# Row, key and r transposes moved from TensorE to the DMA in an RWKV-5 + MLP kernel, with a new order

## Chip, cores and metric

One core of one Trainium2 chip. The metric is the device time of one launch in microseconds. Every instruction's place in its engine's queue is written out by hand in the program, so a time is the result of five queues that run side by side.

## What is computed

Two steps. The first is a linear recurrence (RWKV-5) over 768 positions for 4 batches and 8 heads of 48 channels; the second is a normalisation and a two-layer MLP on the resulting rows of 384 channels.

```python
batch, n_heads, seq, head_dim = (4, 8, 768, 48)
for t in range(S):
    kt, vt, rt = (k[:, :, t].copy(), v[:, :, t].copy(), r[:, :, t].copy())
    cur = np.einsum('bhd,bhe->bhde', u[None] * kt, vt)
    y[:, :, t] = np.einsum('bhd,bhde->bhe', rt, state + cur)
    state = w[None, :, :, None] * state + np.einsum('bhd,bhe->bhde', kt, vt)
...
x = np.ascontiguousarray(attn_out.transpose(0, 2, 1, 3)).reshape(B, S, H * D)
...
xn = (x - mu) / np.sqrt(var + 1e-06) * g_ln
ch = np.maximum(xn @ w_ch1, 0.0) @ w_ch2
return (x + ch).astype(np.float32)
```

Inputs and output are float32; the matrix products run in bf16.

## The kernel before

**Chunks.** The 768 positions of a batch are cut into 6 chunks of 128, so there are 24 chunks (numbered 0 to 23) and as many tiles of 128 rows for the MLP. Within a batch a chunk needs the state `Z` of the chunk before it.

**One chunk, first step.** `LK`, `LR`, `LV` load k, r and v (196.6 KB each, rows of 192 bytes) through SP's DMA queue into rings of ten buffers. `SK` and `SR` (on VectorE or GpSimd) multiply k and r by powers of w and give the bf16 tiles `sck` and `scr`; `CV` gives v in bf16. TensorE needs k and r with channels on the partitions: `TR` turns them, four 128x128 blocks each, into the PSUM tile `tr` (there is one of it, shared with `LT` below), and `TC`, `TCr` or `TCk` copy them to the tile `trs` (a ring of three). `AT` forms the score products, `AM` masks them, `Q` multiplies the turned r and k, `S` forms the state's increment, `ZU`/`ZD` update the state, `Y` forms the output of the chunk and `X` adds the diagonal part `VB`.

**One chunk, second step.** `ST` and `AG` give mean and variance, `XN` the centred row tile `xn` in bf16. `LT` turns it with three 128x128 transposes on TensorE and `XT` copies it to `xT`. Tiles go through the MLP in groups of one or two (`GROUPS`). `UP` is the first layer: for a group of one, 3 PSUM tiles of 12 products each with 128 columns; for a group of two, 6 PSUM tiles of 6 products each with 256 columns. `RL` takes the ReLU. `DN` is the second layer, 3 steps of 4 products with 384 columns for a tile (`DN,4i+d` is tile i, third d). `OT` scales and adds the residual, `STO` stores 196.6 KB through SP's queue.

**Weights.** `LW1,n` loads the third n of the first layer's weights (SP's queue); `SW` scales its three parts; `IW2,n` loads third n of the second layer's weights and converts it, issued from GpSimd's queue. `DN,d` for tile 0 is the first user of third d, so `DN,2` waits for `IW2,2`.

**Transposes by DMA.** For the chunks in `K_BY_DMA` (18 to 23) the k half of `TR` is left out and `TKD` turns `sck` (128x512) with one DMA transpose on SP's queue. `LTD` does the same for `xn` (128x384) but is not in the order before.

**Order.** `PLAN` is the whole schedule: each entry is a step, its index and its engine (v VectorE, s ScalarE, g GpSimd, - fixed). Each engine, and SP's DMA queue, takes its own entries strictly in this order, and a step waits for the data and the free buffers it needs. A DMA on SP's queue that waits keeps all later ones behind it waiting. `DU` and `WU` are products without use, 105 in all, that keep TensorE busy in the first 23 us.

The order before begins like this (up to `DN,2`):

```
MW,0,v WF,0,- TL,0,s MI,0,g MP,0,v WU,13,- MM,0,g LN,0,s LK,0,- ROWSI,0,s WBM,0,- LV,1,-
LR,0,- FK,0,s CV,1,v FR,0,s SK,0,v LK,1,- SR,0,g LR,1,- SK,1,v DU,18,- TR,0,- UW,0,g
WL,0,s LK,2,- SR,1,g TCk,0,s LR,2,- TCr,0,s SK,2,g Q,0,v DU,22,- TR,1,- LV,0,- AT,0,-
TCk,1,s SR,2,v LG,0,- LW1,2,- TCr,1,s AMa,0,v CV,0,g UGC,0,s AMb,0,v DU,13,- TR,2,- S,0,-
Q,1,v TC,2,s Y,0,- AT,1,- CC,0,v ZU,0,v LV,2,- AMa,1,v VB,0,g DU,3,- S,1,- SW,7,s
AMb,1,v LW1,1,- SW,8,s IW2,0,g X,0,v SW,6,s DU,13,- AT,2,- Q,2,v Y,1,- CV,2,g ST,0,v
AG,0,v LW1,0,- CC,1,s XN,0,s RS,0,g ZU,1,v SW,5,s SW,3,v DU,16,- LT,0,- VB,1,g XT,0,v
SW,4,s DU,6,- UP,2,- X,1,v S,2,- RL,2,s SW,2,g ST,1,v UP,1,- SW,0,s SW,1,v IW2,2,g
AG,1,v AM,2,v UP,0,- XN,1,s IW2,1,g LK,3,- LT,1,- RL,1,s CC,2,v XT,1,v LR,3,- DU,1,-
Y,2,- RL,0,s VB,2,g ZU,2,v UP,18,- SK,3,v LV,3,- DN,0,- SR,3,v RL,18,s UP,17,- X,2,v
TR,3,- CV,3,g ST,2,v RL,17,s UP,16,- RS,1,g TC,3,v AG,2,v RL,16,s Q,3,v AT,3,- XN,2,v
RS,2,g AM,3,v S,3,- LT,2,- DN,1,- XT,2,s CC,3,s UP,33,- ZU,3,v LK,4,- DN,2,- LV,6,-
```

Of the kernel before, what the change touches and what calls it, by code (L numbers as in the profile page):

```python
# [13 lines left out]
GROUPS = [1, 1, 1, 1, 1, 1, 1, 1, 2, 2, 2, 2, 2, 2, 1, 1, 1, 1]  # L14
ZPE = [1, 2, 3]
K_BY_DMA = [18, 19, 20, 21, 22, 23]
SLOTS = {'kf': 10, 'rf': 10, 'vf': 10, 'sck': 3, 'scr': 3, 'vv': 4, 'trs': 3, 'q': 2, 'A': 2, 'cc': 4, 'Z': 3, 'ZS': 2, 'Vb': 3, 'x': 13, 'xn': 3, 'xT': 4, 'hT': 4, 'ot': 3}
PLAN = """
MW,0,v WF,0,- TL,0,s MI,0,g MP,0,v WU,13,- MM,0,g LN,0,s LK,0,- ROWSI,0,s WBM,0,- LV,1,-
LR,0,- FK,0,s CV,1,v FR,0,s SK,0,v LK,1,- SR,0,g LR,1,- SK,1,v DU,18,- TR,0,- UW,0,g  # L20
WL,0,s LK,2,- SR,1,g TCk,0,s LR,2,- TCr,0,s SK,2,g Q,0,v DU,22,- TR,1,- LV,0,- AT,0,-
TCk,1,s SR,2,v LG,0,- LW1,2,- TCr,1,s AMa,0,v CV,0,g UGC,0,s AMb,0,v DU,13,- TR,2,- S,0,-
Q,1,v TC,2,s Y,0,- AT,1,- CC,0,v ZU,0,v LV,2,- AMa,1,v VB,0,g DU,3,- S,1,- SW,7,s
AMb,1,v LW1,1,- SW,8,s IW2,0,g X,0,v SW,6,s DU,13,- AT,2,- Q,2,v Y,1,- CV,2,g ST,0,v
AG,0,v LW1,0,- CC,1,s XN,0,s RS,0,g ZU,1,v SW,5,s SW,3,v DU,16,- LT,0,- VB,1,g XT,0,v
SW,4,s DU,6,- UP,2,- X,1,v S,2,- RL,2,s SW,2,g ST,1,v UP,1,- SW,0,s SW,1,v IW2,2,g
AG,1,v AM,2,v UP,0,- XN,1,s IW2,1,g LK,3,- LT,1,- RL,1,s CC,2,v XT,1,v LR,3,- DU,1,-
Y,2,- RL,0,s VB,2,g ZU,2,v UP,18,- SK,3,v LV,3,- DN,0,- SR,3,v RL,18,s UP,17,- X,2,v
TR,3,- CV,3,g ST,2,v RL,17,s UP,16,- RS,1,g TC,3,v AG,2,v RL,16,s Q,3,v AT,3,- XN,2,v
RS,2,g AM,3,v S,3,- LT,2,- DN,1,- XT,2,s CC,3,s UP,33,- ZU,3,v LK,4,- DN,2,- LV,6,-  # L30
VB,3,g UP,32,- OT,0,v Y,3,- SK,4,v LR,4,- DN,4,- RL,32,v RL,33,s DN,5,- CV,6,s LR,5,-
X,3,v SR,4,v DN,6,- LV,4,- ST,3,v TR,4,- SR,5,g UP,34,- OT,1,v LV,5,- TC,4,s AG,3,v
DN,8,- CV,4,v XN,3,g LK,5,- Q,4,v AT,4,- RL,34,s DN,9,- RS,3,g AM,4,v LK,7,- LT,3,-
S,4,- XT,3,s DN,10,- LK,6,- SK,5,v CC,4,s VB,4,g UP,48,- OT,2,v LR,10,- TR,5,- SK,7,v
UP,49,- SK,6,g ZU,4,v RL,48,s LR,6,- TC,5,v Y,4,- CV,5,s DN,12,- RL,49,v LR,12,- ZD,4,g
AT,5,- X,4,v DN,13,- AM,5,v LR,7,- SR,6,g UP,50,- LV,7,- ST,4,v TR,6,- RL,50,s Q,5,v
SR,7,g Y,5,- AG,4,v STO,1,- TC,6,v S,5,- XN,4,s DN,14,- STO,0,- CC,5,v CV,7,s Q,6,v
VB,5,g LT,4,- LV,11,- AT,6,- XT,4,v S,6,- OT,3,v UP,64,- LV,9,- X,5,v CC,6,s UP,66,-
RS,4,g ST,5,v RL,64,s LR,8,- TR,7,- AM,6,v RL,66,s UP,65,- SR,10,g CV,9,s LK,11,- DN,16,-
AG,5,v RL,65,s TC,7,v RS,5,g Y,6,- LR,9,- XN,5,s DN,17,- ZU,6,v VB,6,g Q,7,v LT,5,-  # L40
LK,8,- DN,18,- XT,5,s AT,7,- X,6,v LK,10,- UP,80,- ST,6,v S,7,- SR,8,v RL,80,s LR,14,-
UP,82,- SK,8,g AM,7,v UP,81,- RL,82,s LK,9,- TR,8,- CC,7,s AG,6,v OT,4,v RL,81,s RS,6,g
Y,7,- LK,14,- TC,8,v XN,6,s DN,20,- VB,7,g CV,11,s ZU,7,v LV,8,- LT,6,- DN,21,- Q,8,v
SR,9,g X,7,v XT,6,s AT,8,- LK,15,- SK,9,v DN,22,- CV,8,s UP,96,- ZD,7,g LV,13,- ST,7,v
AM,8,v TR,9,- RL,96,s SK,10,g STO,2,- S,8,- UP,97,- LR,11,- CC,8,s TC,9,v SR,12,g Y,8,-
OT,5,v RL,97,s TR,10,- STO,4,- Q,9,v AT,9,- VB,8,g LK,12,- TC,10,s AG,7,v UP,98,- ZU,8,v
AM,9,v ZD,8,g S,9,- LV,12,- XN,7,s DN,24,- CC,9,s LT,7,- Q,10,v SK,11,g LR,16,- DN,25,-
ZU,9,v RL,98,s X,8,v AT,10,- XT,7,s LV,15,- DN,26,- ZD,9,g ST,8,v UP,114,- AM,10,v LV,10,-
VB,9,g Y,9,- RL,114,s UP,113,- STO,3,- SR,11,g AG,8,v X,9,v XN,8,s LK,13,- UP,112,- CV,10,s
ST,9,v RS,7,g TR,11,- OT,6,v RL,112,s LR,17,- S,10,- AG,9,v TC,11,v RL,113,s SR,14,g Y,10,-  # L50
DN,28,- CC,10,s LR,15,- SK,13,v CV,12,s XN,9,s VB,10,g LT,8,- AT,11,- ZU,10,v LK,17,- DN,29,-
XT,8,s Q,11,v SK,12,g LT,9,- X,10,v DN,30,- LV,16,- XT,9,s AM,11,v S,11,- UP,130,- RS,8,g
LR,13,- UP,129,- CC,11,v OT,7,v RL,130,s ZD,10,g LK,21,- TR,12,- ST,10,v RL,129,s UP,132,- CV,13,v
VB,11,g TC,12,s SR,15,v LK,19,- UP,131,- RL,132,s Y,11,- STO,6,- SR,13,v AT,12,- RL,131,s LK,16,-
Q,12,v UP,128,- AG,10,v X,11,v XN,10,g S,12,- STO,5,- RL,128,s TR,13,- ST,11,v LK,22,- UP,133,-
CV,15,v SR,16,v SK,15,g DN,32,- TC,13,v RL,133,s LR,22,- DN,33,- AG,11,v AM,12,v XN,11,s Q,13,g
LR,21,- LT,10,- CC,12,s DN,34,- XT,10,s ZU,12,v Y,12,- LV,21,- SK,14,g LT,11,- OT,8,v AT,13,-
S,13,- XT,11,v DN,36,- LR,19,- VB,12,g AM,13,v TR,14,- CV,16,g LR,20,- UP,144,- CC,13,v X,12,v
TC,14,s RS,9,g DN,37,- ZU,13,v LV,14,- RL,144,s ST,12,v ZD,13,g UP,145,- STO,7,- UP,148,- RL,145,s
VB,13,g LV,20,- Q,14,v AT,14,- RL,148,s Y,13,- LK,18,- SK,16,v TR,15,- AG,12,v DN,38,- CV,14,v  # L60
TC,15,v LV,22,- UP,149,- OT,9,v XN,12,s TR,16,- LV,23,- Q,15,v RL,149,s DN,40,- X,13,v SR,19,g
# [24 lines left out]
RL,225,s X,22,v DN,76,- ST,22,v UP,241,- DN,77,- RL,241,s AG,22,v RL,226,v XN,22,g Y,23,- DN,78,-
STO,18,- RS,16,g UP,240,- OT,19,v LT,22,- S,23,- RL,240,s DN,80,- XT,22,s DN,81,- CC,23,s VB,23,g
UP,257,- DN,82,- RL,257,s X,23,v STO,19,- UP,256,- OT,20,v UP,242,- ST,23,v DN,84,- AG,23,v RL,242,s
XN,23,g DN,85,- RL,256,s RS,17,g LT,23,- DN,86,- XT,23,v UP,272,- OT,21,v UP,258,- STO,20,- DN,88,-
RL,258,s DN,89,- RL,272,s STO,21,- DN,90,- UP,273,- OT,22,v UP,274,- RL,273,s DN,92,- RL,274,s DN,93,-  # L90
STO,22,- DN,94,- OT,23,v STO,23,-
"""


@with_exitstack
def kernel(
    ctx: ExitStack,
    tc: tile.TileContext,
# [21 lines left out]
    FK = F // P  # L120
# [462 lines left out]
```

## Time and profile before

| | |
|---|---|
| runs | 157.91, 157.92, 160.95 us, median 157.92 |
| profiled execution | 156.55 us, of it 154.4 us span |
| TensorE (PE) | 146.4 us busy, 95% of the span, 1926 products |
| weight loads (PEld) | 118.6 us, 77% |
| VectorE (DVE) | 119.4 us, 77% |
| ScalarE (ACT) | 76.2 us, 49% |
| GpSimd (POOL) | 95.7 us, 62% |
| DMA | 23.51 MB, q1 (SP's and ACT's transfers) 64.5% of 16 engines' span |

The span is the time from the first to the last instruction; the 2.15 us between it and the execution's time lie around it. The median of the runs lies 1.37 us above the profiled execution. "Busy" counts an instruction from its start to its end; products overlap, so the pace of TensorE is read from the distance between starts. In the 40 slices of the span a digit is the busy share of a slice in tenths.

### The profile page before, as it was taken

The page shows a single profiled execution, that of the slowest core. Times are in us where ns is not written, and L with a number is a line of the kernel's source. Part 1 is how long each engine was busy: PE and PEld are TensorE (multiplying, and loading weights), DVE is VectorE, ACT ScalarE, POOL GpSimd, SP SyncE. Part 2 cuts the span into 40 slices and gives each one's busy share as a digit, 9 for nine tenths or more (in the row PEclk, how much of TensorE's full clock was granted, in tenths as well). Part 3 has the DMA queues.
Part 4 walks back from the last instruction along what each step waited for, and adds up shares of the span by engine and source line. Part 5 has one row for each costly group of instructions (what it writes and reads, how often), then busy time and mean ns, then how long its engine had stood idle before and what let it go on. Part 6 is the DMA issues. An engine that isn't in the chain of part 4 may idle for free.

```text
span 154.4 us, 4697 instructions
## 1 busy us (share of the span) xinstructions
PE 146.4 (95%) x1926; PEld 118.6 (77%) x1926; DVE 119.4 (77%) x242; ACT 76.2 (49%) x149; POOL 95.7 (62%) x135
## 2 busy tenths in 40 slices
PE   7689999999899999999999999999999999999990
PEld 4488788868677887979688878877778778878770
DVE  2256989789998999999999999797797769734211
ACT  4526884434155747657535746356455244143330
POOL 3182665356749499995693698798766968333200
PEclk9999999999999999999999999999999999999998
DMA  4999999999999999989899897132153051102111
GB/s 82 192 182 354 349 200 206 210 177 212 226 200 188 199 255 179 257 170 232 170 243 208 176 261 107 51 89 34 51 87 87 0 89 51 51 20 82 56 56 51
DMA packets 84487, 23.51 MB, mean 152 GB/s; under 512 B 79857, under 2 KB 82930, under 8 KB 84466
## 3 DMA queue, kind: packets, MB, share of 16 engines
q1 hardware_dynamic: 83202, 22.03, 64.5%
q0 software_dynamic: 432, 1.18, 4.2%
q8 instruction: 15, 0.25, 0.7%
q10 hardware_dynamic: 832, 0.00, 0.3%
q14 instruction: 6, 0.05, 0.1%
HBM read 18.88 MB, written 4.72 MB: 153 GB/s over the span
## 4 chain that ended last, share of the span: by engine, by line
PE 73%; DVE 16%; DMA 3%; ACT 2%; issue 2%; SPq 1%; POOL 1%; POOLq 0%; DVEq 0%; ACTq 0%
PE o L525 27%; PE hp L497 26%; PE tr L338 5%; PE at L357 4%; DVE A L367 4%; DMA rf<-in_r_dram 3%; PE tr L482 3%; DVE scr L203 2%; PE y L438 2%; PE s L401 2%; PE y L430 2%; PE o L261 2%; DVE x L445 2%; PE s L388 1%; DVE stats L448 1%
## 5 line engine op out<-in xcount | busy, mean ns | idle before, releaser
L513 ACT ACTIVATE hT<-hp 128x512 bf16<-128x512 f32 x68 | 40.0, 597 | 49.5 <-PE hp L497 48.9
L497 PE MATMUL hp<-xT,w_sb 128*128 128x128 bf16 (+1 forms) x648 | 57.2, 237 | 0.3 <-ACT w_sb L306 0.2
L525 PE MATMUL o<-w_sb,hT 128*128 128x384 bf16 x288 | 57.1, 326 | 0.2 <-DVE hT L515 0.2
L497 PEld LDWEIGHTS <-w_sb 128*128 128x128 bf16 x648 | 49.4, 113 | 4.4 <-ACT w_sb L306 0.4
L525 PEld LDWEIGHTS <-hT 128*128 128x128 bf16 x288 | 25.3, 98 | 11.6 <-DVE hT L515 0.4
L367 DVE TENSOR_TENSOR A<-at,mask 128x1024 bf16<-128x1024 f32 (+1 forms) x26 | 29.1, 1127 | 3.3 <-PE at L357 3.3
L420 POOL TENSOR_TENSOR Vb<-vf,cc 128x384 f32<-128x384 f32 x24 | 21.6, 898 | 12.6 <-ACT cc L198 6.7
L203 POOL TENSOR_TENSOR scr<-rf,Fr 128x384 bf16<-128x384 f32 x16 | 16.2, 1019 | 11.7 <-DMA rf<-in_r_dram 8.2
L535 DVE SCALAR_TENSOR_TENSOR ot<-o,rs,x 128x384 f32<-128x384 f32 x24 | 14.7, 611 | 10.3 <-PE o L525 10.2
L445 DVE TENSOR_TENSOR x<-y,Vb 128x384 f32<-128x384 f32 x24 | 13.1, 547 | 4.2 <-POOL Vb L420 3.1
L203 POOL TENSOR_TENSOR Z<-ZS,WLZ 128x384 bf16<-128x384 f32 x13 | 13.6, 1048 | 2.5 <-DVE ZS L414 2.3
L198 ACT COPY trs<-tr 128x512 bf16<-128x512 bf16 (+1 forms) x13 | 10.0, 782 | 10.5 <-PE tr L338 10.5
L448 DVE BATCH_NORM_STATS2 stats<-x 128x6 f32<-128x384 f32 x24 | 13.3, 554 | 0.4
L203 POOL TENSOR_TENSOR sck<-kf,Fk 128x384 bf16<-128x384 f32 x12 | 12.6, 1046 | 0.3 <-PE s L401 0.3
L469 POOL TENSOR_TENSOR rs<-rs,expo 128x1 f32<-128x1 f32 (+1 forms) x18 | 10.9, 603 | 1.5
L338 PE MATMUL tr<-ident,scr 128*128 128x128 bf16 x96 | 9.7, 227 | 1.9 <-POOL scr L203 1.9
L261 PE MATMUL o<-warm 128*128 128x128 bf16 x105 | 10.3, 269 | 1.0 <-DVE warm L226 1.0
L203 DVE TENSOR_TENSOR sck<-kf,Fk 128x384 bf16<-128x384 f32 x12 | 9.6, 799 | 1.4 <-DMA kf<-in_k_dram 1.4
L203 DVE TENSOR_TENSOR q<-trs 128x512 bf16<-128x512 bf16 x18 | 8.8, 489 | 2.4 <-ACT trs L198 2.4
L261 PEld LDWEIGHTS <-warm 128*128 128x128 bf16 x105 | 8.7, 124 | 2.4 <-issue 1.3
L458 ACT ACTIVATE xn<-x,mv 128x384 bf16<-128x384 f32 x15 | 9.2, 613 | 2.5 <-DVE mv L452 2.5
L357 PE MATMUL at<-trs 48*128 48x128 bf16 x192 | 9.8, 222 | 0.4 <-DVE trs L200 0.3
(66 smaller groups left out, 180.2 us busy)
## 6 DMA issues: line engine op xcount, KB each, us to landing
kf<-in_k_dram SPq DMA_DIRECT2D x24, 192.0 KB, 3.9
vf<-in_v_dram SPq DMA_DIRECT2D x24, 192.0 KB, 4.1
rf<-in_r_dram SPq DMA_DIRECT2D x24, 192.0 KB, 3.9
out_dram<-ot SPq DMA_DIRECT2D x24, 192.0 KB, 2.5
w_f<-in_moe_w_ch_dram SPq DMA_DIRECT2D x3, 768.0 KB, 7.3
w_sb<-in_moe_w_ch_dram POOLq DMA_DIRECT2D x3, 384.0 KB, 6.5
trs<-sck SPq DMA_TRANSPOSE x6, 3.6
u_p<-in_u_dram ACTq DMA_DIRECT2D x2, 0.8 KB, 3.1
```

The costliest lines, as they stand in the source:

```text
L203: engines[e].tensor_tensor(out=out, in0=in0, in1=in1, op=ALU.mult)
L261: nc.tensor.matmul(out=warm_ps[0][:, :P], lhsT=warm[:], rhs=warm[:], start=True, stop=True)
L338: nc.tensor.transpose(out=t[:, a * HP + q, :], in_=flat[:, q, :], identity=ident[:])
L357: nc.tensor.matmul(out=t[:, par, q, :], lhsT=trs(i)[p0 : p0 + D, 1, q, :], rhs=trs(i)[p0 : p0 + D, 0, q, :], start=True, stop=True,)
L367: nc.vector.tensor_tensor(out=AA(i)[:, a:b].rearrange("p e q t -> p (e q) t"), in0=psum["at", i][:, a:b].rearrange("p e q t -> p (e q) t") ...
L420: nc.gpsimd.tensor_tensor(out=Vb(i)[:].rearrange("p (h d) -> p h d", h=H), in0=vf(i)[:], in1=cc(i)[:].unsqueeze(2).to_broadcast([P, H, D]) ...
L445: nc.vector.tensor_tensor(out=xx(i)[:], in0=psum["y", i][:, :C], in1=Vb(i)[:], op=ALU.add)
L448: nc.vector.bn_stats(out=stats[i % 4][:], in_=xx(i)[:])
L497: nc.tensor.matmul(out=t[:, a * gw : (a + 1) * gw], lhsT=w1_sb[n][kc][:, fb::FB], rhs=xT(g)[:, kc, :gw], start=(kc == 0), stop=(kc == CK - 1),
L513: nc.scalar.activation(out=o, in_=s, func=ACT.Relu)
L525: nc.tensor.matmul(out=psum["o", i][:, :C], lhsT=hT(g)[:, fk, j * P : (j + 1) * P], rhs=w2_sb[d][:, a, :], start=(fk == 0), stop=(fk == FK ...
L535: nc.vector.scalar_tensor_tensor(out=ot(i)[:], in0=psum["o", i][:, :C], scalar=rs[g][:, j : j + 1], in1=xx(i)[:], op0=ALU.mult, op1=ALU.add,)
```

## The change

- `GROUPS`: tiles 4 to 7, 20 and 21 also go through the MLP in pairs. Before there are 12 groups of one and 6 of two, after 6 of one and 9 of two.
- `K_BY_DMA`: chunks 12 to 23. For these `TR` leaves the order altogether: `TKD` turns k, and the new `TRD` turns r, one DMA transpose each on SP's queue. The copies `TC`/`TCr` of these chunks are gone.
- From tile 8 on, `LTD` takes the place of `LT` and `XT`: one DMA transpose of `xn` on SP's queue.
- `ZPE`: chunk 3 no longer adds its state by a product on TensorE.
- `PLAN` is a new order throughout. SP's queue has 141 DMAs where it had 107: 34 more transposes (12 `TKD`, 12 `TRD`, 16 `LTD`, against 6 `TKD`). Loads of k, r and v are spread over more of the order. The number of `DU`/`WU` products stays 105.

```diff
-GROUPS = [1, 1, 1, 1, 1, 1, 1, 1, 2, 2, 2, 2, 2, 2, 1, 1, 1, 1]
-ZPE = [1, 2, 3]
-K_BY_DMA = [18, 19, 20, 21, 22, 23]
+GROUPS = [1, 1, 1, 1, 2, 2, 2, 2, 2, 2, 2, 2, 2, 1, 1]
+ZPE = [1, 2]
+K_BY_DMA = [12, 13, 14, 15, 16, 17, 18, 19, 20, 21, 22, 23]
...
+    def TRD(i, e):
+        flat = scr(i)[:].rearrange("p h d -> p (h d)")
+        nc.sync.dma_start_transpose(out=trs(i)[:, 0], in_=flat)
```

The order after, its beginning (up to `DN,2`), and two stretches with transposes by DMA:

```
MW,0,v WF,0,- TL,0,s MI,0,g MP,0,v WU,13,- MM,0,g LN,0,s LK,0,- ROWSI,0,s WBM,0,- LR,0,-
FK,0,s LK,1,- FR,0,s SK,0,v SR,0,v LR,1,- WL,0,s DU,17,- TR,0,- LR,3,- UW,0,g TCk,0,s
SK,1,v LV,0,- TCr,0,s SR,1,v Q,0,v DU,12,- AT,0,- LR,2,- SR,3,v TR,1,- AMa,0,v CV,0,g
LV,1,- S,0,- AMb,0,v CC,0,s LK,2,- TCk,1,v DU,3,- Y,0,- SR,2,v CV,1,s TCr,1,v LK,3,-
ZU,0,v DU,10,- AT,1,- VB,0,g SK,2,v LV,2,- Q,1,g AMa,1,v DU,13,- TR,2,- LK,4,- X,0,v
TCk,2,v SK,3,g DU,4,- S,1,- LW1,1,- ST,0,v CC,1,s TCr,2,s AG,0,v CV,2,g AMb,1,v XN,0,s
VB,1,g DU,11,- TR,3,- Q,2,v Y,1,- RS,0,g TC,3,s LG,0,- AT,2,- ZU,1,v LV,3,- AMa,2,v
DU,1,- S,2,- UGC,0,s SW,3,g LT,0,- LR,4,- SW,4,s AMb,2,v XT,0,s X,1,v DU,7,- AT,3,-
LW1,0,- SK,4,g ST,1,v Y,2,- SW,5,s Q,3,v AG,1,v SR,4,v DU,8,- UP,1,- XN,1,s IW2,0,g
CC,2,v CV,3,v LT,1,- VB,2,g LW1,2,- RL,1,s XT,1,v ZU,2,v SW,1,s DU,6,- UP,17,- SW,0,g
X,2,v SW,2,s TR,4,- AM,3,v IW2,1,g S,3,- RL,17,s UP,0,- RS,1,g CC,3,s TC,4,s ZU,3,v
Y,3,- SW,7,v UP,16,- SW,6,g RL,0,s AT,4,- RL,16,s Q,4,v IW2,2,g ST,2,v DN,0,- SW,8,g
AG,2,v XN,2,v VB,3,g UP,2,- AM,4,v UP,18,- ZD,3,g RL,2,s DN,1,- RL,18,v RS,2,g X,3,v
LT,2,- LK,5,- ST,3,v XT,2,s DN,2,- AG,3,v RS,3,g LR,5,- UP,34,- OT,0,v UP,33,- LV,4,-
...
TKD,12,- DN,30,- ST,11,v STO,5,- SR,15,g UP,100,- RL,96,s AG,11,v TKD,13,- OT,7,v XN,11,s AT,12,-
Q,12,v LR,16,- DN,32,- SK,14,g AM,12,v S,12,- LTD,10,- DN,33,- RL,100,s LTD,11,- SR,16,g AT,13,-
CC,12,s Y,12,- DN,34,- SK,15,g ZU,12,v TKD,14,- UP,116,- OT,8,v Q,13,g UP,113,- AM,13,v RL,116,s
...
Q,22,v DN,72,- RL,180,s LTD,20,- RS,12,g S,22,- RL,181,s DN,73,- LTD,21,- SR,23,g AT,22,- CC,22,v
DN,74,- ZU,22,v TKD,23,- AM,22,v UP,192,- ZD,22,g UP,194,- RL,192,s STO,17,- OT,18,v VB,22,g Y,22,-
TRD,23,- UP,195,- DN,76,- X,22,v LV,23,- AT,23,- RL,194,s DN,77,- ST,22,v RL,195,s AM,23,v UP,193,-
```

## The prediction

> **What bounds the kernel now.** I read the page's shares first, then the slices, the chain of waits, the timelines of TensorE and GpSimd, and the groups of `w_f`, `w_sb` and `trs`.
>
> ```profile
> span 154.4 us, 4697 instructions
> PE   7689999999899999999999999999999999999990
> DMA  4999999999999999989899897132153051102111
> ```
>
> TensorE is busy without a hole from slice 12 on. The 16 DMA engines are full until about 92 us and nearly idle afterwards. So removed TensorE work counts in full where nothing takes its place, and DMA added before 92 us competes with loads.
>
> ```profile
> 52.10 0.45 PE tr L338 x8
> 52.92 0.65 PE o L525 x4
> ...
> 80.54 1.31 PE hp L497 x12
> ...
> 95.63 0.22 PE tr L338 x4
> ...
> 117.03 1.32 PE hp L497 x12
> ...
> 132.95 1.34 PE hp L497 x24
> ```
>
> This is the chain of waits (start, length, what): 8 transposes cost 0.45 us of TensorE, 4 cost 0.22, twelve 256-column products of `UP` 1.31, twenty-four of 128 columns 1.34. From 80 us to the end it is almost all TensorE, packed back to back.
>
> ```profile
> 53.41 0.33 PE L482 MATMUL tr<-ident,xn 128*128 128x128 bf16 x3
> 53.58 0.81 PE L525 MATMUL o<-w_sb,hT 128*128 128x384 bf16 x4
> ```
>
> In TensorE's timeline starts matter, not lengths: three row transposes hold it from 53.41 to 53.58, 0.17 us, or 0.056 each, though one lasts 0.22.
>
> **Removed from TensorE.** Chunks 12 to 17 lose 8 transposes each: 6 x 0.45 (starts 55.98 to 56.43) = 2.70. Chunks 18 to 23 lose the 4 of r: 6 x 0.22 = 1.32. Sixteen tiles lose `LT`: 16 x 0.17 = 2.70. Six more tiles go in pairs: a tile costs 3 x 0.67 = 2.01 alone and 1.31 x 1.5 = 1.97 in a pair, 6 x 0.04 = 0.25. `ZPE` loses one 384-column product (20.20 to 20.37), 0.17. Sum 7.1 us. The profile has no hole here for the gain to fall into: with nothing else it would all arrive at the end.
>
> A rule on this price: the Trainium skill (TensorE: Matmul & The Clock Gate, Part 4: PE-mode transpose) puts a 128x128 bf16 transpose at about 275 ns in one kernel's context. The estimate by that page is 120 x 0.275 = 33 us saved; the trace's 0.056 between starts contradicts it, and I keep the trace.
>
> **Removed copies.** 14 fewer copies on ScalarE, 18 fewer steps on VectorE. I cost this at nothing: between 34 and 90 us TensorE is busy 55.22 of 56 us, so at most 0.8 us of waiting is there to gain; after 90 us VectorE has room. Without that cover each copy of 0.4 to 1.0 us would return as gain. More `SK`/`SR` on GpSimd (62% busy) and more `RL` on VectorE are hidden by the same slack.
>
> **The head.** The weight loads stand later in SP's queue. Before, nine loads of k, r, v precede the last `LW1`; after, fourteen.
>
> ```profile
> 19.80 0.69 POOL L310 TENSOR_SCALAR w_sb<-w_f,g_neg 128x512 bf16<-128x512 f32 x1
> 20.44 1.16 POOL L313 DMA_DIRECT2D w_sb<-in_moe_w_ch_dram  x2
> DMA to landing us min/median/max: 5.8/7.3/8.8
> ```
>
> The last third of `w_f` is issued at 10.93 and lands at about 19.7 (8.8 is the longest of the third line, that group's landing times); GpSimd then scales at once (19.80) and only then issues the last two loads of the second layer. After the change `IW2,2` again stands behind a `SW` on GpSimd that needs the last third of `w_f`. Five loads at the full DMA's pace, 196.6 KB / 209 GB/s = 0.94 us (the windows give DMA share 1.00 at 209 GB/s from 34 to 90 us), are 4.7 us: landing 24.4, scaling 0.69, issue at 25.1. Such a load took 5.1 to 7.0 us to land, median 6.5: 30.2 to 32.1, taken 31.6. `DN,2` started at 28.92 and now waits for this: +2.7, bounds +1.3 to +3.2. Before `DN,2` TensorE has done 12.1 us of the useful work, after 12.4, so 0.3 is got back. Net +2.4 (1.0 to 2.9). All products behind `DN,2` wait too, as TensorE takes its steps in order; the dummy products end before.
>
> **Added to SP's queue and the DMA.** 34 more transposes.
>
> ```profile
> L477 SPq DMA_TRANSPOSE trs<-sck x6: 1190/1212/1947, 92.3 to 123.8; - x6
> DMA to landing us min/median/max: 2.4/3.6/4.3
> ```
>
> SP is held 1.21 us for one, and it lands 2.4 us after its issue began at best, 3.6 in the median, though all six ran when loads were over or nearly so. A transpose of `xn` has three blocks of four: estimate 0.91 of issue, 2.1 to land.
>
> How far ahead does the new order place them? I add TensorE's work between a transpose and the first step that needs it. `TRD,23` is followed by `UP,195` and `DN,76`, then `AT,23`: 1.31 us. The later of a chunk's `TKD`/`TRD` has 1.31 (chunks 12, 14, 18, 20, 21, 23), 1.90, 1.96, and 2.9 or more (15, 16, 17, 22). Missing against 2.4: 6 x 1.09 + 0.50 + 0.44 = 7.5 us. The later `LTD` of a group has 1.31, 1.19, 0.97, 1.13, 0.85, 1.02, 0.98, 1.30, 1.32; missing against 2.1: 8.8 us. If SP reached each transpose just when TensorE reached its place in the order, 16.3 us would be lost. If SP runs ahead by 1.3 us, nothing is.
>
> Can it run ahead? From `LTD,8` to `LTD,23` SP issues 82 DMAs: 24 transposes of 1.21, 16 of 0.91, 26 loads, 16 stores. The 40 transposes hold SP 43.6 us. Loads and stores take at least 0.42 and 0.33 (shortest issues in their groups), 16.2; at the full DMA's pace 0.94 each, 39.5. That is 60 to 83 us of SP, and TensorE's work over the same stretch is 72.2 plus about 0.1 at each of 13 `AT`s, 73.5. The middle, 71.5, is 97%. At such a load SP cannot keep a lead, and each `LTD` waits for `XN`, which waits for TensorE's `Y`, with the next loads and stores queued behind. A late store holds `ot`, so `OT` on VectorE and the single PSUM tile `o` and `DN`. So I take half of what is missing: 8.2 us, bounds 0 and 16.3. The nearest row, the 3.6 median, is above the 2.4 used, which speaks against less than half; below zero is excluded, as a wait gives no time back.
>
> On the other side the Trainium skill (Advanced Engine Details and Errata, X-Bar Transpose (TRN2)) holds that transposing DMAs are as fast as ordinary ones, at 350 to 400 GB/s. The estimate by that page is 131 KB in 0.35 us, and no stall: -7.1 + 2.4 = -4.7. The row shows 1.21 us of issue alone, three times the page's whole transfer, so I do not use it.
>
> **Sum.** -7.1 + 2.4 + 8.2 = +3.5, rounded for the copies' small gain to +3.4. The profiled execution becomes 156.55 + 3.4 = 159.95 (span 157.8); the median of the runs shown is 157.92, 1.37 above the profiled one, so 157.92 + 3.4 = 161.3 us, 2.2% slower. The end after the last `DN` (3.5 us) is unchanged.
>
> **Rivals.**
>
> Faster: the transposes are hidden. k and r are scaled 2 to 17 us of TensorE work before their transposes, so SP could lead; it does if the loads' issue costs nearer 0.42 than 0.94. Stalls below 1.5 us: -7.1 + 2.4 + 0.7 = -4.0, 153.9 us. Against it: the 97%, and `XN` ends only about 2 us ahead of its `LTD`.
>
> No change: stalls of 1.5 to 6 us, centre 4: -0.7, 157.2 us. For it: each stall lets SP catch up, so not every shortfall is paid.
>
> Much slower: SP becomes the bound. If the DMA full of small packets holds loads at 0.94 while transposes add their whole issue, SP needs 83.1 us where TensorE needs 73.5: +9.6, and latency on top of 5: -7.1 + 2.4 + 14.6 = +9.9, 167.8 us. It decides once SP's mean time for one of the 82 exceeds 73.5 / 82 = 0.90 us. For it: the DMA row at 9 for 92 us, when only six transposes existed. Against it: a transpose's issue may run while earlier loads drain.
>
> **How the numbers follow.** Forecast (stalls of 6 to 11 us, 159 to 164): 0.42, of which 0.12 within 2%. Hidden: 0.17. No change: 0.22. Much slower: 0.19. Faster by over 2% is 0.17, within 2% 0.22 + 0.12 = 0.34, slower 0.30 + 0.19 = 0.49; 2% is about what a measurement of this kernel can tell from no change. The range takes in most of the hidden case and of the bound by SP: 154 to 169 us.
>
> **What would show it.** Right: 1696 products, transposes 0 to 11 alone on TensorE; `DN,2` starting near 31.6; idle time of about 8 us on TensorE between 60 and 140 us, put down to DMAs into `trs` and `xT`, 0.5 to 1.5 us each; DMA slices at 9 past slice 25; landings of transposes above 3 us while loads run. Wrong: TensorE without holes there (the hidden case), `DN,2` at 29, or SP never waiting for data from 60 to 140 us and stalls of 2 us and more (SP as the bound).

## The result and the profile after

The changed kernel took 168.67 us (median of 4 runs, 167.32 to 170.51), the kernel before beside it 158.01. The ratio is 1.065, with a 95% interval of 1.056 to 1.073: slower by 6.5%, where 2.2% was forecast (161.3 us). The profiled execution took 168.38 us (span 166.5), before 156.55 (span 154.4): +11.8. Some executions are disturbed and take longer: ratios and intervals are of undisturbed ones alone, medians are of all (the 167.42 of the loads from ScalarE's queue is 166.1 without its two disturbed ones), and of three experiments below (rows back on TensorE, w2 alone ahead, two more loads) the profiled execution was a disturbed one, so only their times are used.

The page after: the span, then the busy tenths of TensorE, the clock granted to TensorE and the share of the 16 DMA engines, in tenths, in 40 slices.

```profile
span 166.5 us, 4283 instructions
PE   7959994999999997996795999898797598989991
PEclk9987998799999999999999699999999999999999
DMA  4999999999799798799569785697496697532311
```

Before, TensorE had no hole from slice 12 on; now there are seven digits of 5 to 7 from slice 16 on. The DMA engines, which were nearly idle after slice 25, stay at 4 to 9 up to slice 35. TensorE's waits from 34 to 160 us (line, releaser, us in total, times, longest):

```profile
PE hp L499 <- DMA xT<-xn: 5.2, 6, 1.9
PE at L355 <- DMA trs<-scr: 4.2, 3, 2.3
PE at L355 <- DMA trs<-sck: 1.4, 1, 1.4
```

These are the row turns (`LTD`, waited for by the first `UP` of a group) and the turns of r and k (`TRD`, `TKD`, waited for by `AT`). The list counts only part of what is lost: a wait of the weight load ahead of a product is listed apart, and VectorE, too, waits for `trs`. The whole loss is read from the starts of products. From `DN,2` to the end of the last product TensorE took 121.8 us before, 118.3 of work and 3.5 of stalls, and after 129.9, 110.8 of work and 19.0 of stalls (with rounding). So the account, in profiled executions, is: `DN,2` later by 3.8 (28.92 to 32.73), work less by 7.5, stalls more by 15.5, in sum +11.8.

Not all of the 19.0 is waiting. The granted clock, which before stayed at full speed up to the last slice, is 0.5 in three stretches of some 3.4 us, from 11.1, 28.2 and 93.1 us. The last one lies behind `DN,2`; TensorE is busy all through it, so about 1.7 of the 19.0 us are slower products. It follows a pause of TensorE of 2.29 us (89.5 to 91.8 us); a pause of 1.93 us at 130 us has no such stretch behind it, so when the clock falls is not shown.

What SP did in that time, in its timeline (start, length, line, what; x2 are two in a row):

```profile
79.07 2.50 SPq L471 DMA_TRANSPOSE xT<-xn  x2
81.68 1.21 SPq L475 DMA_TRANSPOSE trs<-sck  x1
82.99 1.21 SPq L479 DMA_TRANSPOSE trs<-scr  x1
84.25 0.57 SPq L317 DMA_DIRECT2D rf<-in_r_dram  x1
84.87 0.58 SPq L544 DMA_DIRECT2D out_dram<-ot  x1
85.50 0.43 SPq L320 DMA_DIRECT2D vf<-in_v_dram  x1
85.97 0.77 SPq L544 DMA_DIRECT2D out_dram<-ot  x1
86.78 1.26 SPq L479 DMA_TRANSPOSE trs<-scr  x1
```

Each issue begins some 0.1 us or less after the end of the last. Between 64 and 146 us SP issues 80 DMAs, about one in 1.02 us: 38 transposes hold it 50.1 us, 26 loads 16.3, 16 stores 9.0, and 6.4 us go in the gaps, of which only 0.5 in a gap above 0.2 us. It is never without work. The chain of waits over the same stretch (start, length, what):

```profile
84.25 0.57 SPq L317
...
84.87 0.58 SPq L544
...
85.50 0.43 SPq L320
...
85.97 0.77 SPq L544
...
86.78 4.98 DMA trs<-scr
91.76 0.04 issue
91.80 0.40 PE at L355 x8
```

The transpose issued at 86.78 is `TRD,14`; the score products of chunk 14 wait for it until 91.80, and what the chain finds ahead of it is not a late input but SP's own queue: a load, a store, a load, a store. Its 4.98 us to landing are the longest of the k and r turns; the median is 3.0.

### The profile page after: what moved, and what is told of

Same layout as the page of the kernel before. It is cut to its first block, busy times and chain, and to the rows that moved or that the text cites. A ratio compares the mean times of both kernels' runs of the same rounds, so it can differ in the third digit from the quotient of the medians.

```text
span 166.5 us, 4283 instructions
## 1 busy us (share of the span) xinstructions
PE 143.8 (86%) x1697; PEld 112.9 (68%) x1697; DVE 117.5 (71%) x224; ACT 70.6 (42%) x136; POOL 97.7 (59%) x135
## 4 chain that ended last, share of the span: by engine, by line
DMA 33%; PE 21%; DVE 13%; SPq 12%; POOL 12%; issue 6%; ACT 1%; POOLq 0%; DVEq 0%; ACTq 0%
PE o L527 11%; DMA trs<-scr 8%; PE hp L499 7%; DMA kf<-in_k_dram 6%; DMA w_sb<-in_moe_w_ch_dram 5%; DMA w_f<-in_moe_w_ch_dram 4%; SPq L314 3%; DMA xT<-xn 3%; POOL scr L201 3%; DVE A L365 3%; SPq L320 2%; POOL sck L201 2%; POOL Vb L418 2%; POOL Z L201 2%; DMA rf<-in_r_dram 2%
## 5 line engine op out<-in xcount | busy, mean ns | idle before, releaser
L499 PE MATMUL hp<-xT,w_sb 128*128 128x256 bf16 (+1 forms) x540 | 57.8, 255 | 6.1 <-DMA xT<-xn 5.2
L515 ACT ACTIVATE hT<-hp 128x512 bf16<-128x512 f32 x60 | 35.6, 596 | 42.4 <-PE hp L499 41.8
L527 PEld LDWEIGHTS <-hT 128*128 128x128 bf16 x288 | 26.3, 99 | 15.5 <-issue 3.3
L537 DVE SCALAR_TENSOR_TENSOR ot<-o,rs,x 128x384 f32<-128x384 f32 x24 | 14.7, 611 | 14.2 <-PE o L527 11.2
L201 POOL TENSOR_TENSOR scr<-rf,Fr 128x384 bf16<-128x384 f32 x18 | 18.3, 1016 | 8.0 <-DMA rf<-in_r_dram 7.7
L201 POOL TENSOR_TENSOR sck<-kf,Fk 128x384 bf16<-128x384 f32 x16 | 17.0, 1063 | 6.7 <-PE y L436 3.7
L201 DVE TENSOR_TENSOR q<-trs 128x512 bf16<-128x512 bf16 x20 | 12.1, 605 | 9.5 <-DMA trs<-scr 5.1
L456 ACT ACTIVATE xn<-x,mv 128x384 bf16<-128x384 f32 x21 | 12.9, 615 | 4.4 <-DVE mv L450 4.4
L355 PEld LDWEIGHTS <-trs 48*128 48x128 bf16 x192 | 6.1, 96 | 12.1 <-issue 7.6
L464 POOL TENSOR_SCALAR rs<-mv 128x2 f32<-128x2 f32 (+1 forms) x15 | 3.2, 215 | 14.6 <-DVE mv L450 13.7
L259 PE MATMUL o<-warm 128*128 128x128 bf16 x105 | 10.7, 269 | 1.0 <-DVE warm L224 1.0
L196 ACT COPY cc<-s 128x8 f32<-128x8 f32 x18 | 2.9, 164 | 19.2 <-PE s L399 14.0
L517 DVE TENSOR_SCALAR hT<-hp 128x512 bf16<-128x512 f32 x12 | 8.2, 683 | 4.0 <-PE hp L499 4.0
```

The costliest lines, as they stand in the source:

```text
L201: engines[e].tensor_tensor(out=out, in0=in0, in1=in1, op=ALU.mult)
L259: nc.tensor.matmul(out=warm_ps[0][:, :P], lhsT=warm[:], rhs=warm[:], start=True, stop=True)
L355: nc.tensor.matmul(out=t[:, par, q, :], lhsT=trs(i)[p0 : p0 + D, 1, q, :], rhs=trs(i)[p0 : p0 + D, 0, q, :], start=True, stop=True,)
L456: nc.scalar.activation(out=xn(i)[:], in_=xx(i)[:], func=ACT.Identity, bias=mean, scale=-1.0)
L499: nc.tensor.matmul(out=t[:, a * gw : (a + 1) * gw], lhsT=w1_sb[n][kc][:, fb::FB], rhs=xT(g)[:, kc, :gw], start=(kc == 0), stop=(kc == CK - 1),
L515: nc.scalar.activation(out=o, in_=s, func=ACT.Relu)
```

## The experiments

Three theories are tried. Q: SP's queue, one DMA after the other, is the bound. D: the order places a transpose too close to its use, and each shortfall is paid whatever SP does. B: the bytes in the 16 DMA engines are the bound. "Stalls" below are counted as above, from `DN,2` to the last product; "SP's waits" are its gaps above 0.2 us between 64 and 146 us.

**Rows back on TensorE.** k and r stay with the DMA.

```diff
-LTD,12,-
+LT,12,- ... XT,12,s          (tiles 8 to 23)
```

> The changed kernel with its 16 row transposes back on TensorE (LT and XT in the place of LTD), k and r still by DMA. Theory Q (SP's queue is the bound: each transpose holds it 1.3 us, and the 14 row transposes between 65 and 146 us hold it 18 us): the queue falls under TensorE's pace, the stalls of about 15.6 us nearly all go, TensorE gains 2.7 us of work: 168.7 - 15.6 + 2.7 + 1.5 left = 157 us (155 to 160). Rival D (the order places transposes too late, each shortfall is paid by itself): only the 8.8 us of the row transposes go: 168.7 - 8.8 + 2.7 = 162.6 us. Rival B (the 16 DMA engines' time is the bound): 16 transposes of some 0.6 us of DMA time less, at most 10 us: about 161 to 165 us.

Measured: 159.09 us, ratio 1.006 (1.001 to 1.011). That is 9.6 us less than after for 16 DMAs less, 2.7 us of TensorE's work put back, and lies within what Q gave (155 to 160), under D's and B's.

**k and r back on TensorE.** The rows stay with the DMA.

```diff
-TRD,14,- ... TKD,14,-
+TR,14,- TCr,14,s TCk,14,v    (chunks 12 to 23)
```

> The changed kernel with k and r of all chunks turned on TensorE (TR, TCr, TCk where the later of TKD and TRD stood), rows still by DMA. Theory Q: 24 transposes of 1.3 us less on SP, 31 us of 81: the queue is no bound, TensorE gains 12 x 0.45 = 5.4 us: 168.7 - 15.6 + 5.4 + 2 for the late copies = 160 us (157 to 163). Rival D: only the 7.5 us of k and r go: 168.7 - 7.5 + 5.4 = 166.6 us. Rival B: 24 transposes of 0.75 us of DMA time less: 158 to 162 us.

Measured: 165.92 us, ratio 1.054 (1.043 to 1.064). Q's 157 to 163 is missed. The time is D's number, but not for D's reason. TensorE's waits from 34 to 160 us:

```profile
PE o L528 <- DVE ot L538: 2.5, 5, 0.7
PE o L528 <- ACT hT L516: 2.5, 2, 1.3
PE at L356 <- DVE A L366: 0.8, 1, 0.8
PE hp L500 <- DMA xT<-xn: 0.5, 1, 0.5
```

The row turns, alone on the DMA, cost TensorE 0.5 us where after has 5.2, though they stand where they stood. What is new is a wait of the second layer for ScalarE and VectorE, into whose queues this edit puts 24 copies at places of my choice. As TensorE is held up elsewhere, some of the rows' shortfall may be hidden. So the run doesn't price the rows, and it speaks against D for them without settling it.

**Thin loads.** Left out: of the loads of chunks 12 to 23, seven heads of eight.

```diff
-nc.sync.dma_start(out=kf(i)[:], in_=chunk_src(k, i))
+n = 1 if i >= 12 else H
+nc.sync.dma_start(out=kf(i)[:, :n], in_=chunk_src(k, i)[:, :n])   (r and v too)
```

> The changed kernel, but the loads of k, r and v for chunks 12 to 23 bring one head of eight (the other seven heads keep what an earlier chunk left; output is not the reference's). The number of DMAs on SP and the transposes stay; the load's DMA time falls from 1.0 us to some 0.15. Theory Q: SP still issues 82 DMAs with 50 us in transposes; a load holds it 0.58 us at any size: 163 to 168 us, a gain of 0 to 5 from landings that come sooner. Rival B: some 31 us of DMA time go from 60 to 140 us, the stalls vanish: 153 to 156 us. Rival D: no change, 166 to 169 us.

Measured: 163.40 us, ratio 1.037 (1.028 to 1.045). The DMA share from 64 to 146 us falls from 0.80 to 0.45, and 14.6 us of stalls remain: B alone is out, and the time is at the lower end of Q's 163 to 168. SP waits 4.6 us. TensorE's waits for k and r turns fall from 5.6 to 1.8 us, those for row turns rise from 5.2 to 6.8.

**Late loads from ScalarE's queue.** The 26 loads that stand behind `LTD,8` are issued there.

```diff
+q = nc.scalar if f"LK{i}" in late else nc.sync
-nc.sync.dma_start(out=kf(i)[:], in_=chunk_src(k, i))
+q.dma_start(out=kf(i)[:], in_=chunk_src(k, i))                    (r and v too)
```

> The changed kernel with the 26 loads that stand behind the first row transpose issued from ScalarE's DMA queue, at the same places of the order. DMA work and transposes are the same; SP loses 16.3 us of issue and the gaps, ScalarE (42% busy) gains 26 x 0.6 = 16 us. Theory Q: SP needs 64 us for what took 81, TensorE's 73.5 us set the pace again: 156 to 160 us, up to 163 if ScalarE is held by loads that wait for a free buffer. Rival B and rival D: no gain, 166 to 170 us.

Measured: 167.42 us, ratio 1.053 (1.041 to 1.066). SP now waits 15.8 us, and yet the stalls are 17.0. Q in its bare form is out as well. The time from issue to landing of the k and r turns, here:

```profile
L484 SPq DMA_TRANSPOSE trs<-scr x12: 1188/1206/2457, 66.6 to 138.9; - x12
DMA to landing us min/median/max: 2.4/3.6/6.8
```

In after it was 2.4/3.0/5.0 (below). What SP no longer holds, the engines seem to: the loads are the same bytes in the same 16 engines. The other candidate is ScalarE, which the 26 issues now hold for 12.5 us and behind which many of SP's waits stand. The next run tests both. The Trainium skill (DMA: Bandwidth & Descriptors, Rules for kernel authors) says just this of spreading DMAs over several queues, that it saves issue time only; the run agrees.

**Both at once.** Left out: the same seven heads of eight.

```diff
 q = nc.scalar if f"LK{i}" in late else nc.sync
+n = 1 if i >= 12 else H
+q.dma_start(out=kf(i)[:, :n], in_=chunk_src(k, i)[:, :n])
```

> Leaves out part of the loads: as in the thin-load run those of chunks 12 to 23 bring one head of eight; and as in the other run the 26 late ones are issued from ACT's queue instead of SP's. Loads from ACT alone left 17.0 us of stalls with SP waiting 15.8 us, thin loads alone 14.6 us with SP issuing nearly all the time. Theory Q with bytes (SP's holds come first; once SP is free, the bytes of loads ahead of a transpose in the DMA engines take their place): with both gone the k and r stalls vanish and the row turns keep some 4 to 8 us: 156 to 161 us. Theory D (order alone): 162 to 167. If a second issuing queue by itself delays the transposes: 163 to 167.

Measured: 156.93 us, ratio 0.993 (0.988 to 0.998). Of after's ratio of 1.065, thin loads had taken 0.028, the other queue 0.012, both together 0.072. Landing of the k and r turns:

```profile
L487 SPq DMA_TRANSPOSE trs<-scr x12: 1188/1204/2016, 66.2 to 130.4; - x12
DMA to landing us min/median/max: 2.4/2.5/4.9
```

With SP's queue and the engines both free, all 40 transposes, where the changed order puts them, cost 7.7 us of stalls instead of 19.0. ScalarE still issues the 26 loads (9.7 us), so its issues are not what kept the gain away in the run before. And the places were not the main fault. Q with bytes was right (156 to 161).

**One DMA for k and r.** They share a buffer and are turned by one DMA of 8 blocks, where the second of the two stood. The output is the reference's.

```diff
-    sck = ring("sck", [P, H, DP], BF16)
-    scr = ring("scr", [P, H, DP], BF16)
+    sc = ring("sck", [P, 2, H, DP], BF16)
...
-        flat = scr(i)[:].rearrange("p h d -> p (h d)")
-        nc.sync.dma_start_transpose(out=trs(i)[:, 0], in_=flat)
+        flat = sc(i)[:].rearrange("p a h d -> p (a h d)")
+        nc.sync.dma_start_transpose(out=trs(i)[:].rearrange("p a q t -> p (a q) t"), in_=flat)
```

> Order as after, but the keys and r of a chunk share one buffer and are turned by one DMA of 8 blocks, issued where the second of the two stood: 12 DMA transposes for k and r instead of 24. Theory Q (SP's in-order queue is full, 1.05 us per DMA, so k and r turns are late however early the order has them): a transpose held SP's queue for 1.21 us with 3 blocks and with 4, so if the hold doesn't grow with blocks, some 12 x 1.25 = 15 us of SP's time come free between LTD,8 and LTD,23, and the stall at the score products (6.7 us in after) falls to 2 us or less: 161 to 165 us. Were the hold to grow with the blocks (2.4 us for 8): 167.5 to 170. Theory D (the steps of the order stand too close, and each shortfall is paid whatever SP does): 167 to 170, since no consumer is moved.

Measured: 159.08 us, ratio 1.007 (1.002 to 1.013). It moves the same bytes and takes 12 DMAs off SP, and 9.6 of after's 10.7 us are gone, a larger gain than Q had given (161 to 165). The turns of after, where a DMA has 4 blocks (instruction's min/median/max in ns, first and last start):

```profile
L479 SPq DMA_TRANSPOSE trs<-scr x12: 1188/1237/2346, 68.9 to 142.4; - x12
L475 SPq DMA_TRANSPOSE trs<-sck x12: 1188/1216/1742, 75.2 to 140.5; - x12
...
DMA to landing us min/median/max: 2.4/3.0/5.0
```

and of this run, where it has 8:

```profile
L479 SPq DMA_TRANSPOSE trs<-sck x12: 1231/1248/2527, 70.8 to 131.7; - x12
...
DMA to landing us min/median/max: 3.1/3.7/5.5
```

Twice the blocks hold SP 1.25 us instead of 1.22 to 1.24, and land 0.7 us later. SP's waits are 11.2 us, the stalls 9.4: `AT` waits for DMA 0.8 us (5.6 in after), `UP` for rows still 3.7.

**Another order, same DMAs.** Behind a point 20 steps ahead of `LTD,8` the steps are put in an order found by search, in which the turns stand farther from their uses. Chunk 14, TensorE's and SP's entries between its r turn and its `AT`:

```diff
-TRD,14,- DN,38,- TKD,15,- UP,115,- LTD,12,- AT,14,-
+TRD,14,- AT,13,- TKD,15,- S,13,- UP,99,- Y,12,- TRD,15,- DN,28,- DN,29,- DN,30,- UP,96,- Y,13,- AT,14,-
```

> The same DMAs and the same work as after, and the same order up to 20 steps ahead of the first row turn; behind it the steps are put in another order, in which a k and r pair stands 7 TensorE steps ahead of its score product in the mean instead of 3.5, and a row turn 5.7 steps ahead of its first hidden product instead of 3.6. Theory D (distance in the order is what is missing): the stalls at score and hidden products, 13.8 us in after, fall by 5 to 8 us: 160.5 to 163.7 us. Theory Q (SP issues without a break from 65 to 146 us, so a transpose placed earlier only pushes another DMA later): little, 166 to 169. From my replay of both with the durations of after's trace: 4.7 us less, that is 164.

Measured: 167.80 us, ratio 1.067 (1.058 to 1.076), no gain; my replay's 164 was a miss, Q's 166 to 169 held. Twice the distance in the order, and 18.2 us of stalls:

```profile
PE hp L499 <- DMA xT<-xn: 4.0, 2, 2.1
PE s L386 <- DVE q L201: 2.0, 1, 2.0
PE at L355 <- DMA trs<-sck: 1.8, 3, 1.3
```

What became of the distance is told by SP's lead: from the start of a turn's issue to the time when TensorE reaches that turn's place in the order. For k and r its mean is 1.4 us in after, and -0.3 here: SP now issues a turn after TensorE has gone past its place. In the merged run it is 2.7. The full queue handed out one DMA in about 1.05 us here too (78 between 64 and 146 us); standing earlier in the order did not get the turns issued earlier.

**The other order on top of the merge.**

```diff
-TRD,14,- DN,38,- TRD,15,- UP,115,- LTD,12,- AT,14,-
+TRD,14,- DN,28,- DN,29,- Y,12,- UP,101,- AT,13,- DN,30,- UP,99,- UP,96,- S,13,- AT,14,-
```

> The merged turn of k and r (one DMA of 8 blocks a chunk, as in the run at 159.1 us), and the steps re-ordered from 20 ahead of the first row turn on. Re-ordering without the merge moved 168.7 to 167.8. If distance in the order counts once SP's queue has room (11 us of waits there in the merged run): the 9.4 us of stalls fall by 3 or so: 155.5 to 157.5 us. If order never counts: 158.5 to 160.

Measured: 160.23 us, ratio 1.014 (1.009 to 1.020), against 1.007 without it: no gain either. TensorE's waits for rows fell from 3.7 to 1.6 us, but 2.4 came at `DN` for VectorE (`ot` 1.7, `hT` 0.7) and 1.6 at `S` for `q`. The search traded one wait for another.

**Rows from tile 18 only.** Merged k and r; tiles 8 to 17 back on TensorE (10 `LT`, +1.7 us of work). Once in a searched order, once in after's own.

```diff
-LTD,12,-
+LT,12,- ... XT,12,s          (tiles 8 to 17)
```

> A version meant to beat both: k and r of chunks 12 to 23 by the merged DMA, rows by DMA from tile 18 only (10 row turns back on TensorE, 10 x 0.17 = 1.7 us), the steps re-ordered from 20 ahead of the first row turn on; the head is that of after. TensorE's work behind DN,2 is 110.8 + 1.7 = 112.5; from DN,2 at 32.7 and 4 to 6 us of stalls the span is 153.5 to 155.5 and the time 155 to 157.5. If row turns by DMA cost in the order whatever stands around them: 158 to 160.

> The version of 155.2 us without its re-ordering: after's order, k and r of chunks 12 to 23 by the merged DMA, rows by DMA from tile 18 on, the row turns of tiles 8 to 17 as LT and XT where the DMA stood. With all rows by DMA this was 159.1 us and 4.3 us of stalls at row turns. If what is won comes from taking rows off the DMA (stalls down by 3 for 1.7 us of TensorE): 157 to 159. If the re-ordering is what won: 159 to 161; if nothing of it did: 154.5 to 156.5.

Measured: 155.15 us, ratio 0.983 (0.973 to 0.993), in the searched order; 155.62, ratio 0.988 (0.982 to 0.993), in after's own. Both intervals lie below the kernel before, by 1 to 2%, and the order adds nothing that they tell. The page of the second, and TensorE's waits:

```profile
span 154.0 us, 4296 instructions
PE   7969988699999999999999999999999998999990
DMA  4999999999959979998899916995893888611311
```

```profile
PE hp L500 <- DMA xT<-xn: 0.4, 1, 0.4
PE at L356 <- DMA trs<-sck: 0.3, 2, 0.2
```

SP waits 24.6 us and leads TensorE by 3.9 us in the mean of the k and r turns; the holes are closed, with 4.7 us of stalls behind `DN,2` at 32.76. The places of the k and r turns are after's, which the forecast had found 7.5 us short.

**Before's order with the new DMAs.** Head, groups and order of before; merged turns where `TR` stood, rows by DMA from tile 18 where `LT` stood. Once so, twice re-ordered.

```diff
-TR,16,- ... TC,16,s
+TRD,16,-                     (chunks 12 to 23)
-LT,18,- ... XT,18,v
+LTD,18,-                     (tiles 18 to 23)
```

> The head and the groups of before (DN,2 at 28.9 instead of 32.7), with k and r of chunks 12 to 23 by the merged DMA and rows by DMA from tile 18, the steps re-ordered from 20 ahead of row turn 8. TensorE's work behind DN,2: 118.3 less 6 x 0.45 (TR 12 to 17), 6 x 0.22 (r's half of 18 to 23) and 6 x 0.17 (LT) = 113.3; with 4 to 6 us of stalls the span is 150 to 152 and the time 151.5 to 154, under every kernel here. If the head's gain is given back by the smaller groups' stalls: 154 to 157.

> The head, groups and order of before; k and r of chunks 12 to 23 by the merged DMA, put where the TensorE turn stood (behind both scalings), and rows by DMA from tile 18 where LT stood. So SP has room (some 20 DMAs fewer than after), but each turn stands as near to its use as a TensorE turn did. Theory D in its bare form (with SP free, a turn that stands too near is still paid): 18 turns at 1 us or so each, 160 to 167. Theory Q alone (SP's fullness is all): 151.5 to 156.

> The same DMAs and the same head as the run beside it, the steps re-ordered from 20 ahead of row turn 8, so that the turns stand earlier. An earlier try at this, in which two chunks' keys were turned before they were scaled, so that the output is not the reference's, took 155.6 us: its head was at 29.1, its stalls 7.3. With the turns behind the scalings: 153 to 156.5 under both theories. Against the run beside it this shows what distance is worth once SP's queue has room: 5 us or more by D, under 1.5 by Q.

Measured: 155.62 us, ratio 0.987 (0.980 to 0.994), for the first; 171.13, ratio 1.095 (1.085 to 1.105), in before's near order; 156.00, ratio 0.992 (0.986 to 0.997), re-ordered. In the last two, chunk 18's r is turned after chunk 21's scaling has overwritten it; the work is the same, but that turn waits for another scaling. In the first, the keys of chunks 21 and 23 are turned before they are scaled, so these two turns wait for less than they must. None of the three gives the reference's output, and the first shows no valid gain. Here D is right: in the near order SP issues 52 DMAs from 64 to 146 us and waits 30 us, and there are still 24.1 us of stalls; the same DMAs in a wider order have 8.3. So the order counts, by 15 us, once SP has room; the time lies above D's 160 to 167 too. Some 6 of the 24.1 us are a granted clock of 0.5 (80.1 to 86.9, 107.4 to 110.8 and 134.7 to 138.1 us), each time during or just after a pause of TensorE of 2.3 us or more; the wider order, without such a pause, has none of it. Much of the rest is not where the DMA's data goes. TensorE's waits in the near order, and VectorE's timeline:

```profile
PE hp L496 <- DMA xT<-xn: 3.9, 3, 2.3
PE y L437 <- DVE A L366: 3.8, 1, 3.8
PE y L429 <- POOL Z L202: 2.9, 1, 2.9
```

```profile
75.50 0.92 DVE L199 CAST vv<-vf 128x384 bf16<-128x384 f32 x1
79.67 0.56 DVE L202 TENSOR_TENSOR sck<-rf,Fr 128x384 bf16<-128x384 f32 x1 [3.25 <-DMA trs<-sck]
80.14 0.18 DVE L451 BATCH_NORM_AGGREGATE mv<-stats 128x2 f32<-128x6 f32 x1
80.24 1.19 DVE L366 TENSOR_TENSOR A<-at,mask 128x1024 bf16<-128x1024 f32 x1
```

VectorE idles 3.25 us for the DMA that turns chunk 13. What waits is not a user of the turned data but `SR,16`: it writes the scaled tile that this turn still reads, as the ring has three buffers. The mask step `AM,12`, ready earlier, stands behind it in VectorE's order, so `Y,12` waits 3.8 us. The third line of the waits is the same on GpSimd: `SR,20` waits for the turn of chunk 17, and `ZD,15` stands behind it. So a turn can stand too near to the next writer of its buffer as well as to its use; a deeper ring was not tried.

**Weights in the head.** First w2's three loads alone ahead, then w1 and w2, then two more loads of k ahead of w2.

```diff
+RS,0,g IW2,0,g IW2,1,g IW2,2,g               (first and second)
+LV,2,- LW1,1,- LW1,0,- LW1,2,-               (second only)
+LX,0,- LX,1,- LK,5,-                         (third, order otherwise as after)
```

> After, with one edit in the head: the three GpSimd DMAs that bring w2 are issued one after the other at about 18 us, instead of at 20.6, 23.1 and 25.3 us behind weight scalings on the same engine. Head theory (the whole lateness of the first down products, DN,2 at 32.7 us against 28.9 before, comes of w2, whose last two parts landed at 30.3 and 32.4): w2 lands some 4 us earlier, DN,2 moves to 29 to 30.5, 165.5 to 167 us. Rival (the loads, which share the DMA engines there, or the first hidden products set it): DN,2 stays at 32 or more and the time at 168 to 169.5.

> After, with the head's weights ahead of its late loads: the three w1 DMAs stand directly behind the load of v's chunk 2 on SP's queue (ahead of the loads of k's chunk 4, v's chunk 3 and r's chunk 4), and the three w2 DMAs on GpSimd's queue at about 18 us. With w2 alone moved, it landed at 24.2, 27.6 and 30.2 us, but the last w1 part, which had landed at 24.6, came at 30.4, and DN,2 at 36.3. Head theory (the bytes ahead of the last weight set DN,2): both weights are down by 27 us, DN,2 moves from 32.7 to 29 to 30.5, and the time falls by as much: 165 to 166.5 us. Rival (the delayed loads and their chunks' products take the place): 167.5 to 169.5.

> After, with two more loads of the same size (k's chunk 5 again, into tiles that nobody reads), put just ahead of the load of k's chunk 5 on SP's queue; w2 is issued behind them on GpSimd's queue as before. Byte theory of the head (the loads that stand ahead of w2 in the 16 DMA engines set DN,2, which w2's last part releases): two loads at 0.8 us of the engines each push w2's landing and DN,2 from 32.7 to 34 to 34.6, and the time to 170 to 171. Rival (w2 is late by its own issue, at 20.6, 23.1 and 25.3 us on GpSimd): DN,2 stays at 32.5 to 33 and the time at 168 to 169.3.

Measured: 167.24 us, ratio 1.060 (1.048 to 1.071); 174.64, ratio 1.107 (1.097 to 1.116); 168.13, ratio 1.065 (1.057 to 1.074). The first and third can't be told from after. The second is 6 us slower, and its `DN,2` starts at 38.49: the load of v's chunk 3, put behind the weights, landed at 28.2 instead of 19.2, and the granted clock was 0.50 from 24.1 to 34.4 us. How much is due to each is not shown. So the weights are not late for want of a better place among the loads that I found, and two extra loads did not cost what bytes alone would. What sets the head beyond w2's issue stays open.

**Two searches from further ahead.** Rows on TensorE with the merged turn, re-ordered from `DN,2` on; and before's own work, re-ordered from the start.

```diff
-LTD,12,- ... TRD,14,- ... TKD,14,-                          (after)
+LT,12,- XT,12,s ... TRD,14,-                                (rows on TensorE, merged, re-ordered)
-... LR,3,- ... LV,3,- ... LK,4,- DN,2,-                     (before)
+... LW1,0,- LV,3,- LR,4,- ... LV,4,- LK,5,- LR,5,- UP,2,-   (before, re-ordered)
```

> The head of after; row turns all on TensorE (16 LT of 0.17 us, +2.7 us of TensorE, and their copies) ; keys and r of chunks 12 to 23 by one DMA of 8 blocks per chunk; all steps from the first DN,2 on re-ordered by a search with the durations of the traces. If both theories hold together (late by distance for the rows, by SP's queue for k and r): the stalls nearly vanish and the time is TensorE's work, 118.3 - 7.5 + 2.7 = 113.5 behind DN,2 at 32.7 with 3 to 6 us of stalls left and 12 us of tail and launch: 152 to 156 us, under before. If a DMA of 8 blocks costs twice one of 4, or the TensorE stalls come from something not yet seen (the copies, buffers): 157 to 163.

> The kernel before with its steps put in another order by the same search, nothing else changed. Its TensorE had 3.5 us of stalls behind DN,2 at 28.9. If a new order alone is worth something: 154.5 to 157; if the search only trades one stall for another, as it did with all turns by DMA: 157.5 to 160.

Measured: 159.95 us, ratio 1.015 (1.009 to 1.020), and 162.09, ratio 1.028 (1.022 to 1.034): the first misses its 152 to 156 (it lies in the range of its rivals, 157 to 163), the second both of its ranges. The first put two steps of `UP` and three more loads ahead of `DN,2`, which started at 35.22. The second's `DN,2` went from 28.92 to 33.03, as late as in after, and its stalls from 3.5 to 6.9 us. It pulls loads of chunks 4 and 5 ahead of the first hidden products, as the change does with two of chunk 4. Neither came below the kernel before.

## Why the prediction was wrong

**Work removed, -7.1.** Measured -7.5 behind `DN,2`. Right. The 275 ns of one transpose that the prediction held against its 0.056 between starts is a length, as is the trace's 0.22; it does not contradict the pace, which alone tells what is saved.

**Copies at nothing.** No run speaks against it.

**Head, +2.4.** Mechanism right, size off: `IW2,2` was issued at 25.29 (25.1 forecast) and landed at 32.44, 7.15 us later, where 6.5 was taken from rows of 5.1 to 7.0; `DN,2` started at 32.73 instead of 31.6. That is +3.8, or 3.5 net of the 0.3, beyond the bound of 2.9. The last third of `w_f` landed at 24.55, as forecast (24.4). In this profile TensorE waits 2.27 us for the first third of w2 at `DN,0` and then runs at a clock of 0.5 from 28.2 to 31.6 us, so at `DN,2` no wait is left to see; with a clock of 1.0 there (the merged run) `DN,2` waits 1.07 us for its third of w2, landed at 32.56, and starts at 32.61.

**Stalls, +8.2.** This step failed: measured +15.5 (about 1.7 of it the lower clock), near the upper bound of 16.3. The failing choice was "half of what is missing", made from a load of SP that I put at the middle of 60 to 83 us, 97% of TensorE's work. The terms of that load were mis-sized. A row turn of three blocks was estimated at 0.91 of issue and took a median of 1.21, as one of four blocks does (mean 1.29 with the long ones): 5 us over 14. A k or r turn took 1.33 in the mean, not 1.21: 3 us over 24. The gaps of 0.08 us between issues, 6.4 us in all, were not counted. Loads and stores were 25.3 us, inside their bounds. The sum is 81.8 us for 80 DMAs where 71.5 was forecast for 82: 111% of TensorE's 73.5, near the upper end, and 1.02 us per DMA is past the 0.90 from which the rival decides. In place of a queue that half hides the shortfalls, the runs showed a queue that is full: with 12 DMAs fewer and the same bytes the stalls are 9.4 us.

**Landing.** The prediction went by 2.1 for rows and 2.4 for k and r; the shortest were 2.3 and 2.4, the medians 2.9 and 3.0. The row that I named as speaking against less than half, 3.6, was the better guide.

**The rivals.** What happened is "SP becomes the bound", put at 167.8 and 0.19; 168.67 was measured. Its sign was named too: SP never waiting for data, and stalls of 2 us and more. Its mechanism was half the story: the runs show two limits in a row, SP's holds and the loads' bytes behind them, of which the one or the other lifted alone leaves more than half of the loss (ratios 1.037 and 1.053, after 1.065) and both together give it all back (0.993). Fewer turns in the queue do nearly as much with the loads as they are (1.006 and 1.007). That its time came within 0.9 us is in part luck: it had the head at 2.4 (measured 3.8) and the stalls at 14.6 (15.5), +9.9 in profiled executions where +11.8 was measured. The hidden case, at 153.9, is nearly reached (155.6) with the change's own places for k and r, once SP has 19 DMAs fewer in that stretch, with ten row turns back on TensorE.

**The page on X-bar speed.** The Trainium skill (Advanced Engine Details and Errata, X-Bar Transpose (TRN2)) was set aside for the 1.21 us row. The runs bear this out: the hold per DMA decided. As an estimate, 4 more blocks (131 KB) took 0.7 us more to land at best, 187 GB/s, half of the page's 350 to 400; as loads shared the engines, this is no test of the page's rate.

## What to carry to other kernels

Here an in-order queue ran out of DMAs before bytes: one of twice the size held it hardly longer. Add up a queue's holds and the gaps between them over the stretch where the new DMAs go, at the durations of the trace; where they reach the time of the bounding engine, do not count on half of the loss being hidden. In this case it paid first to make each DMA larger (two tiles in one buffer, one transpose), then to think of the order; a new order in front of the full queue only moved the lateness. With room in the queue the order counted by 15 us, and the next writer of a turn's buffer belongs to what must stand far enough away. A look at the waits, not at the time alone, told apart two causes that gave the same number.

## What was not expected of the hardware

- A DMA transpose held SP's queue 1.21 us with 3 blocks of 128x128, 1.22 to 1.24 with 4, 1.25 with 8 (medians). The landing grew: shortest 2.3, 2.4, 3.1 us.
- With the late loads issued from ScalarE's queue, transposes issued from SP's landed later: the median of the k and r turns went from 3.0 to 3.6 us, the longest from 5.0 to 6.8; with an eighth of the bytes in these loads the median was 2.5.
- TensorE's granted clock was 0.5 for 3.4 us in the changed kernel (93.1 us) and 13.6 us in the near order, during or after pauses of TensorE of 2.3 to 3.8 us; before, without such pauses, it stayed full up to the end.
